# Loading K and V of a decode attention in rows of 32 KB instead of 16 KB per partition

## The chip, the cores and the metric

The kernel runs on one core of one Trainium2 chip. The metric is device time in microseconds (us) of one execution; the profile's span is about 2 us shorter than that time. Inputs and weights are bf16.

## The reference

Two decode attentions, A and B, each of one token, are computed and their outputs put side by side. A looks at the last 2048 positions of its cache, B at all 8192.

```python
B, Sq, D = 1, 1, 576
Hq, Hkv, Sk, Dh = 32, 16, 8192, 128          # two query heads share a K/V head
# x [1,1,576], k_cache and v_cache [1,16,8192,128], wq [576,4096], wo [4096,576], for A and for B
W = min(4096, max(256, Sk // 4))             # 2048, for A only
q = (x @ wq) in heads;  k, v = the caches (A: only the last W positions)
p = softmax(q k^T * Dh ** -0.5);  o = p v
out = o in one row @ wo                      # [1,1,576] for A, the same for B, concatenated
```

The work is moving bytes: 8 MB each of K and V for A, 32 MB each for B, and 18 MB of weights; in all 102.76 MB have to come out of HBM. (Sizes of arrays, slots and rows are in units of 1024: 98 such MB are 102.76 million bytes. The profile's totals and GB/s are in units of 1000.)

## The kernel before

SP (SyncE) issues all large loads, in order. K and V have four slots each; a slot holds 16 KB in each of 128 partitions (2 MB). A slot for B holds two heads, 64 rows of HBM each, a row being 64 positions of one head (16 KB in one piece); for A four heads and 32 rows each. Neighbouring partitions belong to different heads, so the load's source has the dimensions (row, head, bytes of a row): 64 x 2 for B, 32 x 4 for A.

```python
SLOT = 8192; NS = 4; TS = 64                 # elements of a slot in a partition; slots; positions of a row
G = [4, 2]                                   # heads of a slot: A, B

def load_kv(arrs, g, s, slots, name, after=()):
    ...
    ch = 128 // G[P] * TS
    def src():
        return arrs[P][0, i * G[P]:(i + 1) * G[P], r0:r0 + ch, :].rearrange("g (p t) d -> p g (t d)", t=TS)
    load(slots[:, s, :], src, [(name, s)], "%s%d" % (name, s), after)
```

PE (TensorE) transposes K in blocks of 128x128, ACT and DVE bring them to SBUF (`kt`), PE multiplies them with the queries. Columns of `kt` of different heads alternate, so the products read every second column:

```python
def k_scores(g, u, place):                   # one half slot, 1 MB of K
    for e in range(2):
        for j in range(4):
            rhs = kt[:, u % NKT, j * 1024:(j + 1) * 1024].rearrange("d (x g) -> d x g", g=2)[:, :, e]
            pe.matmul(sacc[32 * j:32 * j + 32, 512 * half:512 * half + 512], lhsT=qst[...], rhs=rhs, ...)
```

Then follow softmax of a chunk, its transposes, the products with V out of the V slots, and at the end the product with wo. A K slot is free for its next load when it is transposed; a V slot when its products are done, which needs the chunk's softmax. `x` arrives in two small loads issued by ACT.

## Time and profile before

| | before |
|---|---|
| time, median of 4 runs | 249.97 us |
| span of the profiled run | 247.7 us |
| bytes, rate over the span | 102.76 MB, 415 GB/s |
| busy: PE, ACT, DVE | 68%, 35%, 33% |

Five lines of the page of the kernel before. The first three divide the span into 40 slices: the granted clock of TensorE in tenths, the mean busy share of the 16 DMA engines in tenths (9 is 90% or more), and GB/s. Then all packets, and the queue that carries SP's loads with the share of 16 engines' span that its packets took.

```profile
PEclk9999959999799979998899955999858755557555
DMA  7999999999999999999999999999999999999993
GB/s 270 406 433 431 430 431 421 426 423 429 431 425 429 426 421 431 422 431 434 423 429 429 423 431 429 426 437 426 429 429 423 431 426 429 434 427 427 421 406 138
DMA packets 8235, 102.92 MB, mean 416 GB/s; under 512 B 1184, under 2 KB 1312, under 8 KB 2080
...
q1 hardware_dynamic: 7936, 102.77, 98.0%
```

All DMA engines are busy from the second slice to the last but one, at 421 to 437 GB/s in nearly every slice. That is the bound.

The costliest groups of PE in the kernel before, by form (count | busy us, mean ns of one | idle before and what ended it):

```profile
L466 PE MATMUL ktps<-ident,kslots 128*128 128x128 bf16 x1280 | 85.1, 230 | 12.4 <-PEq L214 12.4
L557 PE MATMUL opsum<-vslots,ptm 128*32 128x128 bf16 x1280 | 28.1, 262 | 28.0 <-PEq L214 23.7 <-issue 4.3
L486 PE MATMUL sacc<-kt,qst 128*32 128x512 bf16 x320 | 25.3, 392 | 1.8 <-PEq L214 1.8
```

The issues of the kernel before, from the DMA view (count, KB each, median us from issue to landing):

```profile
kslots<-in_B_k_cache_dram SPq DMA_DIRECT2D x16, 2048.0 KB, 19.6
vslots<-in_B_v_cache_dram SPq DMA_DIRECT2D x16, 2048.0 KB, 18.4
```

At the 428 GB/s of the stretch from 100 to 200 us, a 2 MB load (2.10 million bytes) moves in 4.9 us, so a load issued 19 us before it lands has three others ahead of it: the queue is never near empty.

The trace also holds a record of every DMA packet (start, duration, bytes, queue). Wherever this document gives packet times, they are summed up from these records. One row of a partition is one packet. Before, 5632 packets of 16384 bytes (5120 of K and V, 512 of wq) took 614 ns in the median, 616.9 on average, and the engines lacked data for only 0.4 us between the first and the last data packet.

### The profile page before, as it was taken

The numbers are of one execution on the slowest core, as the hardware profiler recorded it, in microseconds if no ns is written. First come the engines' busy times: TensorE is split into PE (matmuls) and PEld (weight loads), VectorE is DVE, ScalarE is ACT, GpSimd is POOL, SyncE is SP. The second block draws the span as 40 slices with busy tenths as digits, with TensorE's granted clock in tenths as the row PEclk, the third lists the DMA queues.
The fourth block names the chain that finished last, engine by engine and source line by source line (L and its number), as shares of the span: only waits on it lengthen the run. The fifth ranks groups of instructions, "written<-read, shape, count | busy, mean of one in ns | idle before, by whom it ended". The sixth has DMA issues, their size and how long they took to land. (4 is left out here: it accounts for less than half of the span.)

```text
span 247.7 us, 7505 instructions
## 1 busy us (share of the span) xinstructions
PE 169.6 (68%) x3406; PEld 132.3 (53%) x3406; DVE 81.0 (33%) x152; ACT 87.1 (35%) x92; POOL 12.9 (5%) x49
## 2 busy tenths in 40 slices
PE   0193589994999559995999638998345144685634
PEld 0031288763877458864878428785244142584522
DVE  0001225554555017564555122655004004204000
ACT  2000047767478009786578004775200000000000
POOL 7501000000000000000000000000000000000000
PEclk9999959999799979998899955999858755557555
DMA  7999999999999999999999999999999999999993
GB/s 270 406 433 431 430 431 421 426 423 429 431 425 429 426 421 431 422 431 434 423 429 429 423 431 429 426 437 426 429 429 423 431 426 429 434 427 427 421 406 138
DMA packets 8235, 102.92 MB, mean 416 GB/s; under 512 B 1184, under 2 KB 1312, under 8 KB 2080
## 3 DMA queue, kind: packets, MB, share of 16 engines
q1 hardware_dynamic: 7936, 102.77, 98.0%
q8 instruction: 8, 0.13, 0.2%
q10 hardware_dynamic: 288, 0.00, 0.1%
q14 instruction: 3, 0.02, 0.0%
HBM read 102.76 MB, written 0.00 MB: 415 GB/s over the span
## 5 line engine op out<-in xcount | busy, mean ns | idle before, releaser
L472 ACT ACTIVATE kt<-ktps 128x1024 bf16<-128x1024 bf16 x80 | 77.9, 1021 | 54.5 <-PE ktps L466 54.4
L466 PEld LDWEIGHTS ktps<-ident,kslots 128*128 128x128 bf16 x1280 | 78.9, 103 | 27.9 <-issue 27.9
L466 PE MATMUL ktps<-ident,kslots 128*128 128x128 bf16 x1280 | 85.1, 230 | 12.4 <-PEq L214 12.4
L475 DVE COPY kt<-ktps 128x1024 bf16<-128x1024 bf16 x80 | 55.2, 691 | 53.7 <-PE ktps L466 53.6
L557 PE MATMUL opsum<-vslots,ptm 128*32 128x128 bf16 x1280 | 28.1, 262 | 28.0 <-PEq L214 23.7
L557 PEld LDWEIGHTS opsum<-vslots,ptm 128*32 128x32 bf16 x1280 | 25.3, 119 | 31.6 <-issue 31.6
L486 PE MATMUL sacc<-kt,qst 128*32 128x512 bf16 x320 | 25.3, 392 | 1.8 <-PEq L214 1.8
L566 DVE TENSOR_TENSOR diag<-opsum,rows 128x512 f32<-128x512 f32 x5 | 3.5, 691 | 55.9 <-PE opsum L557 55.9
L425 PE MATMUL opsum<-vslots,xpad 128*32 128x512 bf16 x64 | 8.2, 489 | 14.8 <-DVE xpad L410 12.1
L599 ACT ACTIVATE stat<-stat 128x1 f32<-128x1 f32 (+1 forms) x2 | 0.6, 294 | 37.2 <-DVE stat L597 37.2
L425 PEld LDWEIGHTS opsum<-vslots,xpad 128*32 128x32 bf16 x64 | 2.3, 119 | 17.6 <-issue 13.1
L457 POOL COPY qst<-qtm 128x64 bf16<-128x64 bf16 x20 | 4.5, 236 | 123.2 <-PE sacc L486 113.5
L646 PE MATMUL ktps<-kslots,opj 128*32 128x144 bf16 x184 | 6.1, 326 | 5.8 <-DMA kslots<-in_B_wo_dram 3.9
L486 PEld LDWEIGHTS sacc<-kt,qst 128*32 128x32 bf16 x320 | 5.1, 94 | 8.2 <-issue 4.4
L431 ACT ACTIVATE qrow<-opsum 128x512 bf16<-128x512 f32 x2 | 1.2, 597 | 23.1 <-PE misc L425 23.1
L523 ACT ACTIVATE psb<-sacc,stat 128x2048 bf16<-128x2048 f32 x3 | 5.9, 1967 | 8.5 <-DVE stat L517 8.5
L646 PEld LDWEIGHTS ktps<-kslots,opj 128*32 128x32 bf16 x184 | 5.2, 145 | 6.4 <-DMA kslots<-in_B_wo_dram 4.2
L425 PE MATMUL misc<-vslots,xpad 128*32 128x512 bf16 x64 | 8.2, 487 | 0.0
L630 PE MATMUL misc<-acc,pick 128*128 128x32 f32 x16 | 3.8, 404 | 3.6 <-DVE acc L624 2.9
L433 DVE CAST qrow<-misc 128x512 bf16<-128x512 f32 x2 | 1.4, 692 | 14.6 <-PE misc L425 14.6
L652 DVE CAST outsb<-ktps 128x144 bf16<-128x144 f32 x2 | 0.6, 307 | 16.0 <-PE ktps L646 16.0
L630 PEld LDWEIGHTS misc<-acc,pick 128*128 128x128 f32 x16 | 3.6, 328 | 3.8 <-DVE acc L624 3.0
(66 smaller groups left out, 62.1 us busy)
## 6 DMA issues: line engine op xcount, KB each, us to landing
kslots<-in_B_k_cache_dram SPq DMA_DIRECT2D x16, 2048.0 KB, 19.6
vslots<-in_B_v_cache_dram SPq DMA_DIRECT2D x16, 2048.0 KB, 18.4
kslots<-in_A_k_cache_dram SPq DMA_DIRECT2D x4, 2048.0 KB, 29.8
vslots<-in_A_v_cache_dram SPq DMA_DIRECT2D x4, 2048.0 KB, 23.5
vslots<-in_A_wq_dram SPq DMA_DIRECT2D x2, 2048.0 KB, 9.9
vslots<-in_B_wq_dram SPq DMA_DIRECT2D x2, 2048.0 KB, 19.6
kslots<-in_A_wo_dram SPq DMA_DIRECT2D x2, 2016.0 KB, 23.8
kslots<-in_B_wo_dram SPq DMA_DIRECT2D x1, 2016.0 KB, 31.2
```

The source lines that it names most:

```text
L425: ins = pe.matmul(qps[c][32 * j:32 * j + 32, :], lhsT=xpad[:, P, x, :], rhs=src[:, o:o + 512], start=(u == 0), stop=(u == WQ_UNITS - 1))
L433: add("dve", lambda dve: dve.tensor_copy(qrow[:, 512:1024], misc[:, :]), reads=[B_M], writes=[("qrow", 1)])
L457: add("pool", lambda pool: pool.tensor_copy(qst[:, s * 64:(s + 1) * 64], qtm[:, o:o + 64]), reads=[("qtm", KIND[g])], writes=[("qst", s)], ...
L466: ins = pe.matmul(ktps_bf[q][:, t * 128:(t + 1) * 128], lhsT=kslots[:, s, o:o + 128], rhs=ident[:, :], start=True, stop=True, is_transpose ...
L472: add("act", lambda act, q=q, dst=dst: act.activation(dst, ktps_bf[q], ACT.Copy), reads=[("bank", q)], writes=[("kt", u % NKT, q)], tag="e ...
L475: add("dve", lambda dve, q=q, dst=dst: dve.tensor_copy(dst, ktps_bf[q]), reads=[("bank", q)], writes=[("kt", u % NKT, q)], tag="e%d%d" % ( ...
L486: ins = pe.matmul(sacc[32 * j:32 * j + 32, 512 * half:512 * half + 512], lhsT=qst[:, s * 64 + e * 32:s * 64 + e * 32 + 32], rhs=rhs, start ...
L523: return act.activation(psb[:, :].rearrange("p (x g) -> p x g", g=2), src, ACT.Exp, bias=st(P, C_NB + k), scale=SCALE, accum_out=st(P, C_L ...
L557: ins = pe.matmul(opsum[32 * j:32 * j + 32, s * DH:(s + 1) * DH], lhsT=ptm[:, o:o + 32], rhs=vslots[:, s, b * 128:(b + 1) * 128], start=(u ...
L566: return dve.tensor_tensor(diag[:, g % 2, :, :], opsum[:, :].rearrange("p (s d) -> p d s", s=NS), m, ALU.mult)
L630: ins = pe.matmul(misc[:, 0:32], lhsT=pick[:, r, :], rhs=acc[:, d, 32 * r:32 * r + 32], start=(r == 0), stop=(r == 3))
L646: ins = pe.matmul(ktps[P][32 * j:32 * j + 32, 0:OUTW], lhsT=opj[:, P, jj:jj + 32], rhs=view[:, o:o + OUTW], start=(jj == 0), stop=(jj == H ...
```

## The change

A packet costs a little more than its bytes (before, 178 ns for 4608 bytes and 614 ns for 16384, in the median), so longer rows should be cheaper. The change goes to 128 positions (32 KB) for each row and halves the number of packets. To keep the chunks small it takes eight heads into a slot, 16 rows of each; there are two slots for K and two for V, of 4 MB each. wq comes in rows of 36 KB, one load for A and one for B. The chunks of A and B have the same shape, which removes masks and zeroing. The eight heads of a slot are sorted out by extra products ("spread") that write P^T in the form the V products need.

The core of the diff (cut):

```diff
-SLOT = 8192
+SLOT = 16384
-NS = 4
+NS = 2
+NG = 8
-TS = 64
+TS = 128
+CH = 128 // NG * TS
 ...
-            return arrs[P][0, i * G[P]:(i + 1) * G[P], r0:r0 + ch, :].rearrange("g (p t) d -> p g (t d)", t=TS)
+            return arrs[P][0, s * NG:(s + 1) * NG, r0:r0 + CH, :].rearrange("g (p t) d -> p g (t d)", t=TS)
 ...
-            for e in range(2):
+            for g in range(NG):
                 for j in range(4):
-                    rhs = kt[:, u % NKT, j * 1024:(j + 1) * 1024].rearrange("d (x g) -> d x g", g=2)[:, :, e]
+                    o = k0 * UNIT + j * 2048
+                    rhs = kt[:, o:o + 2048].rearrange("d (x g) -> d x g", g=NG)[:, :, g]
 ...
+    def softmax_spread(i, loop):
+        pe.matmul(dst[:, :], lhsT=spread[:, i, :], rhs=pt0[:, :], ...)      # eight for each chunk
+        dve.tensor_tensor(<ptm>, <dst>, <hmask>, ALU.mult)
 ...
+    ORDER = [                                   # order of issue: K, V slots and wo
+        [("k", 0), ("k", 1), ("v", 0)],
+        [("k", 2), ("k", 3), ("v", 1)],
+        [("k", 4), ("v", 2), ("k", 5), ("v", 3)],
 ...
```

## The prediction

> **What bounds it now.** The DMA engines. The page's slices show them at 90% or more from the second slice on; the main queue's packets took 98.0% of 16 engines' span. In the trace's packet records the 16 engines have data in flight for 242.3 us of the 242.7 us between first and last data packet: no starvation. PE (68%), ACT (35%) and DVE (33%) matter only where they free a slot late. The chain of waits ends in B_wo's load.
>
> **What it can gain.** Only cost per packet. Median packet times: 4608 B 178 ns, 9216 B 352 ns, 16384 B 614 ns: a line of 7.4 ns + 0.0370 ns per byte. By it (estimates) 32768 B takes 1221 ns instead of 2 x 614, 36864 B takes 1373 ns. Over all K, V, wq and wo rows, with fewer completion packets, that is about 1.7 us less per engine (0.7%). [...]this trace already runs at 421 to 437 per slice, so over 2% is out of reach.
>
> **What it can lose: an empty queue.** Before, 2 MB loads are issued a median 18 to 20 us before they land. After, 4 MB loads (9.8 us each) go into four slots; slots come free later, and SP issues in order. Release against need:
>
> - x: its packets came one per 0.61 us data packet on each engine. Behind 36 KB packets both x need about 25-30 us (estimate; 14.1 before), so the B query ends at about 37 us. Slot k0 is ready at 35-36 us: costs PE 1-2 us, not the DMA.
> - K stage: a 1 MB transpose unit takes 1.96 us PE, 2 x 1.02 us ACT, 2 x 0.69 us DVE. The eight spread evictions (0.69 us each, like the 128x512 TENSOR_TENSOR) make two units DVE-bound, about 4.2 us each. A K stage is then 26-27 us, in 39 us of DMA.
> - Chunk 1's round: PE work is continuous there; V slot 0 is released about 28 us after the first K lands, and its refill is needed just then. No margin. A first-pass instruction fetch, like the 4.3 us "issue" wait in the middle of V before, falls here: 0-6 us idle, say 2.
> - Later chunks: 3-4 us of margin, none lost.
> - First wo load: reuses K slot 0, but is issued after K slot 1's last transposes (9.3 us after landing, 10-11 if PE is cold), while only one 9.8 us load is queued behind that K. Issue to first packet takes 1 us: 1-2.5 us idle. [...]64 transposes took 6.5 us at 31.9 us, 4.05 at 91.8.
>
> PE, ACT and DVE savings are off the critical path. The tail (3 us) stays.
>
> **Sum.** 249.9 - 1.7 + about 3 idle = 251.2 us; 80% range 248.2 to 255. Faster by over 2%: 1%; within 2%: 88%; slower by over 2%: 11%.
>
> **Right if** packets of 32768 B take about 1.22 us, busy engine time falls 1.5-2 us, and the DMA row dips near 95 us and near 205 us. **Wrong if** there is no dip (then about 248.2), if large packets are no cheaper per byte, if instruction fetches behind 32 KB packets take much longer, or if the late x starves the early K loads (then 255 or more).

Two clauses are cut from it, as they did not come from this case's runs. Neither held a term of the sum, which stays 249.9 - 1.7 + about 3 = 251.2 us; but "over 2% is out of reach" now rests on the estimated 0.7% alone. What some of its words stand for in the trace of the kernel before: "cold" is a granted clock of 0.54 over the 64 transposes that took 6.5 us, against 0.92 over those that took 4.05; the "completion packets" are taken to be the 888 packets of 4 bytes in the queue of SP's loads, 9 ns each (488 after); and the 1 us from issue to first packet is the first load, issued at 0.73 us, with its first data packet at 1.75.

## More of the kernel before

The score products (L486) keep PE busy for 25.3 us in all. They overlap one another (320 of 392 ns would make 125 us), so the mean of one says less than the busy time.

## The result, and the profile after

| | before | after |
|---|---|---|
| time, median of 4 runs | 249.97 us | 450.2 us (444.81 to 454.31) |
| ratio of the fast runs | | 1.794, 95% interval 1.777 to 1.810 |
| span of the profiled run | 247.7 us | 446.9 us |
| packets of K and V (before: with 512 of wq): count, mean | 16384 bytes: 5632, 0.617 us | 32768 bytes: 2560, 2.43 us |
| wq packets of 36864 bytes | none | 256, median 1.364 us |

The ratio is the mean time of the fast runs of one kernel over that of the other's of the same rounds, so not quite the ratio of the medians in the table. One run of the kernel after (454.31 us) is slow and left out of it.

The same lines of the page of the kernel after:

```profile
PEclk9978698795999659757975965797596579856566
DMA  9999999999999999999999999999999998899994
GB/s 360 432 241 218 205 224 199 224 201 223 221 220 214 226 220 209 229 226 214 217 224 211 214 232 202 223 217 214 223 214 217 226 214 268 204 209 214 204 389 170
DMA packets 4636, 102.94 MB, mean 230 GB/s; under 512 B 784, under 2 KB 912, under 8 KB 1296
...
q1 hardware_dynamic: 4336, 102.76, 97.8%
```

The engines are as busy as before, and move half as much: 430 GB/s while wq comes in (the second slice), about 215 GB/s as soon as K does, 389 again at the end when only wo is left. A busy DMA engine is an engine with a packet under way, not an engine at its rate: the DMA row alone would have called this kernel healthy, and the GB/s row beneath it shows the fault at a glance.

PE's costliest groups in the kernel after, by form:

```profile
L470 PE MATMUL ktps<-ident,kv 128*128 128x128 bf16 x1280 | 101.6, 248 | 128.2 <-PEq L215 121.3 <-issue 6.8
L495 PE MATMUL sacc<-kt,qst 128*32 128x256 bf16 x640 | 75.6, 632 | 0.0
L550 PE MATMUL opsum<-kv,ptm 128*32 128x128 bf16 x1280 | 24.6, 247 | 34.0 <-PEq L215 24.0 <-issue 9.9
```

A second surprise: the score products (L495) move as many columns as before (640 x 256 against 320 x 512) and take 75.6 us instead of 25.3.

The issues of the kernel after, from its page:

```profile
kv<-in_B_k_cache_dram SPq DMA_DIRECT2D x8, 4096.0 KB, 53.1
kv<-in_B_v_cache_dram SPq DMA_DIRECT2D x8, 4096.0 KB, 40.4
```

Where the 200 us went is a simple sum over the packet records. K and V now take 2560 packets of 2428 ns where twice 616.9 ns was the old price of the same bytes: 2560 x (2428 - 1234) ns / 16 engines = 191 us. Engines without a packet between first and last data grew from 0.4 to 5.3 us, 5 us more. wo rows that shared the queue with the last V loads are about 3 us slower for each engine (16128 bytes 707 ns on average against 606 before, 20736 bytes 959 where the line of the prediction gives 775). So the question is why a packet of 32768 bytes takes 2.43 us, when one of 36864 bytes, in the same run, takes 1.36.

### The profile page after: what moved, and what is told of

It reads as the page before. It is cut to its first block, busy times and chain, and to the rows that moved or that the text cites. A ratio compares the mean times of both kernels' runs of the same rounds, so it can differ in the third digit from the quotient of the medians.

```text
span 446.9 us, 8083 instructions
## 1 busy us (share of the span) xinstructions
PE 236.4 (53%) x3716; PEld 159.6 (36%) x3716; DVE 101.7 (23%) x197; ACT 86.8 (19%) x96; POOL 15.4 (3%) x41
## 5 line engine op out<-in xcount | busy, mean ns | idle before, releaser
L470 PE MATMUL ktps<-ident,kv 128*128 128x128 bf16 x1280 | 101.6, 248 | 128.2 <-PEq L215 121.3
L470 PEld LDWEIGHTS ktps<-ident,kv 128*128 128x128 bf16 x1280 | 95.4, 114 | 142.8 <-issue 139.2
L495 PE MATMUL sacc<-kt,qst 128*32 128x256 bf16 x640 | 75.6, 632 | 0.0
L550 PE MATMUL opsum<-kv,ptm 128*32 128x128 bf16 x1280 | 24.6, 247 | 34.0 <-PEq L215 24.0
L550 PEld LDWEIGHTS opsum<-kv,ptm 128*32 128x32 bf16 x1280 | 23.5, 112 | 37.0 <-issue 37.0
L495 PEld LDWEIGHTS sacc<-kt,qst 128*32 128x32 bf16 x640 | 20.4, 113 | 43.0 <-issue 42.0
L430 PE MATMUL opsum<-kv,xpad 128*32 128x512 bf16 x72 | 9.7, 514 | 24.2 <-DVE xpad L415 24.2
L540 DVE TENSOR_TENSOR ptm<-misc,hmask 128x512 bf16<-128x512 f32 x24 | 16.4, 682 | 3.5 <-PE misc L534 3.3
L540 DVE TENSOR_TENSOR ptm<-ptps,hmask 128x512 bf16<-128x512 f32 x24 | 16.3, 678 | 0.0
L534 PE MATMUL misc<-pt,spread 128*128 128x512 bf16 x24 | 9.6, 398 | 4.2 <-PEq L215 2.7
```

Source lines behind the costliest of these rows:

```text
L430: ins = pe.matmul(qps[c][32 * j:32 * j + 32, :], lhsT=xpad[:, P, x, :], rhs=src[:, o:o + 512], start=(u == 0), stop=(u == WQ_UNITS - 1))
L470: ins = pe.matmul(ktps_bf[q][:, t * 128:(t + 1) * 128], lhsT=kslots[s][:, o:o + 128], rhs=ident[:, :], start=True, stop=True, is_transpose ...
L495: ins = pe.matmul(sacc[32 * j:32 * j + 32, 256 * h:256 * h + 256], lhsT=qst[:, s * 256 + g * 32:s * 256 + g * 32 + 32], rhs=rhs, start=(a ...
L534: add("pe", lambda pe: pe.matmul(dst[:, :], lhsT=spread[:, i, :], rhs=pt0[:, :], start=True, stop=True), reads=["pt0", "spread"], writes=[ ...
L540: return dve.tensor_tensor(to, dst[:, :].rearrange("p (f n h) -> p f n h", f=4, n=4), m, ALU.mult)
L550: ins = pe.matmul(opsum[32 * j:32 * j + 32, s * DH:(s + 1) * DH], lhsT=ptm[:, o:o + 32], rhs=vslots[s][:, b * 128:(b + 1) * 128], start=(m ...
```

## The experiments

All are single looks (one timed run and a profile each, so their state is unknown), as nearly every question here is one of tens of per cent; the kernel before, run beside each of them, gave 249.63 to 250.04 us. Kernels "wrong on purpose" read other data than they should, for the sake of the timing. One more caution: the comparison with the reference cannot see every error in this problem. The kernel of `e5_flat_only` below pairs scores with the wrong keys and was still reported as correct. That fits scores so small that softmax is nearly flat, but no run here measured that. And the theories speak of which rows an engine moves and in what order; that is assumed throughout, as the packet records name no engine.

### 1. Address pattern, packet size, or number of heads

`m1_sweep` has no computation, only loads from one cache in 21 patterns:

```python
for dims, row, gap, off in TESTS:              # dims: the source's outer dimensions, outermost first
    for r in range(4):                         # four loads, then wait for all of them
        sp.dma_start(<buffer r, 128 partitions>, <source with dims, row>)
    sp.wait_ge(s_dma, n)
```

> No computation, wrong output on purpose: 21 address patterns, each four loads of about 4 MB, one pattern after the other, only the packet records count. Measured after the change: 32768-byte packets took 2.43 us on average instead of the 1.22 us predicted, and the 36864-byte packets of wq took 1.36 us, their predicted time. Theory A (address spacing): the 16 engines start their rows 32 KB apart in HBM and read 32 KB on[...]; then the pattern as after repeats about 2.5 us; a row spacing of 36 KB, and probably 33 or 34 KB, brings 1.22 us for the same packet size; and the same addresses read in 16 KB pieces stay slow (about 1.2 us a piece instead of 0.61). Theory B (packet size): a 32768-byte packet is itself slow; then every pattern with 32 KB packets takes about 2.5 us, whatever the spacing, and the 16 KB pieces of the same addresses take 0.61 us. Theory C (eight heads 2 MB apart, one after the other on an engine): then a head spacing of 2 MB + 4 KB or of 512 KB brings 1.22 us and 36 KB row spacing alone does not.

The kernel had a slip: its unit was half of what was meant, so all rows and row spacings were half as long as the text says (16 KB for "32 KB"); the head spacing of 2 MB was right. The comparison between patterns does not suffer. Some of the 21, with the real sizes:

| source: outer dimensions, row | spacing of rows; of heads | packet, median | rate |
|---|---|---|---|
| 16 x 8, 16 KB | 16 KB; 2 MB | 1276 ns | 212 GB/s |
| the same addresses, in pieces of 8 KB | 16 KB; 2 MB | 614 ns | 219 GB/s |
| 16 x 8, 8 KB | 16 KB; 2 MB | 612 ns | 223 GB/s |
| 16 x 8, 16 KB | 18 KB; 2 MB | 1265 ns | 212 GB/s |
| 16 x 8, 16 KB | 64 KB; 2 MB | 1255 ns | 212 GB/s |
| 16 x 8, 16 KB | 16 KB; 2 MB + 4 KB | 1274 ns | 211 GB/s |
| 16 x 8, 16 KB | 16 KB; 256 KB (all contiguous) | 1273 ns | 214 GB/s |
| 32 x 4, 16 KB | 16 KB; 2 MB | 611 ns | 412 GB/s |
| 64 x 2, 8 KB | 8 KB; 2 MB | 309 ns | 392 GB/s |
| 128, 16 KB | 16 KB | 611 ns | 402 GB/s |

All three theories fall. Neither the size of the packets, nor the spacing of rows, nor that of heads brought any of the slow patterns out of 210 to 226 GB/s. All 16 slow patterns have 16 as the source's outermost dimension; the five fast ones have 32, 64 or 128.

In `e1_half_rows` each slot is filled by two loads of 16 KB rows:

```diff
-        load(slots[s], src, [(name, s)], "%s%d" % (name, s), after)
+        def halves(sp):
+            a, d = src(), slots[s]
+            return [sp.dma_start(d[:, h * 8192:(h + 1) * 8192], a[:, :, h * 8192:(h + 1) * 8192]) for h in range(2)]
```

> The kernel after the change, with each K or V slot filled by two loads of 16 KB per partition (first halves of all rows, then second halves), correct result. Theory B (packet size) expects 16384-byte packets of 0.61 us and about 250 us in all. Theory A (spacing) leaves it open: rows still stand 32 KB apart but an engine reads only 16 KB before it changes the head, as the A loads of the kernel before did at full rate; if the overlap of 16 KB is still too regular it expects 1.2 us packets and about 450 us.

Correct, 425.0 us; packets of 16384 bytes took 1193 ns in the median, against 614 before. Packet size is not the cause. (The A loads of the kernel before, which the text names, ran at 421 to 431 GB/s between 25 and 65 us.)

`e2_pitch36` takes rows 36 KB apart:

```diff
-            return arrs[P][0, s * NG:(s + 1) * NG, r0:r0 + CH, :].rearrange("g (p t) d -> p g (t d)", t=TS)
+            return bass.AP(..., ap=[[18 * 512, 16], [SK * DH, NG], [1, TS * DH]])    # elements; wrong on purpose
```

> The kernel after the change with the 16 rows of a head taken 36 KB apart instead of 32 KB (wrong result on purpose: rows overlap other rows and some keys are left out), packets of 32768 bytes kept. Theory A (spacing): packets of about 1.22 us, and the time the prediction gave, 248 to 255 us. Theories B (packet size) and C (heads 2 MB apart): about 450 us still.

453.6 us and packets of 2500 ns: no help. Theory A was a supposition that no run had shown. Here rows 36 KB apart are as slow as rows 32 KB apart (2500 ns against 2495 in the kernel after, in the median), and in `m1_sweep` heads 2 MB + 4 KB apart as slow as heads 2 MB apart (1274 ns against 1276), so it is out.

### 2. Which partitions the load writes

Theory D is the next supposition: packets that are written to certain partitions at the same moment hold one another up, and an outermost dimension of 16 brings such partitions together. Which partitions these are, and which engine writes them, was assumed; no run here shows it. The main test needs no such assumption: if the place of writing counts, one and the same source must run at different rates to different partitions. By rival E, to which the outermost dimension of 16 is slow in itself, it must not.

`m2_ports`, in the right units, and `e3_rows32`, the kernel after with other rows:

```diff
-            return arrs[P][0, s * NG:(s + 1) * NG, r0:r0 + CH, :].rearrange("g (p t) d -> p g (t d)", t=TS)
+            r1 = min(r0, SK - 2 * CH)           # wrong on purpose: 32 rows of four heads
+            return arrs[P][0, s * NG:s * NG + 4, r1:r1 + 2 * CH, :].rearrange("g (p t) d -> p g (t d)", t=TS)
```

In `m2_ports`, s is the step from one written partition to the next, for 16 rows of one and the same source. In its last pattern two small loads, of 16 and 48 rows, go ahead of the 16 x 8 loads and are meant to put the engines out of step.

> No computation, wrong output on purpose; only the packet records count, with packets of 32768 bytes (16384 in one pattern). The first sweep dropped theories A, B and C: only patterns whose source has an outermost dimension of 16 were slow. Theory D[...]. It expects: loads of 16 x 8 rows 2.44 us a packet and about 215 GB/s at row spacings of 32 and 36 KB; 32 x 4, 64 x 2 and 128 rows 1.22 us and over 400 GB/s. [...] Last, [...]16 x 8 loads take 1.22 us a packet although nothing of their pattern differs from the first. Rival E (the outermost dimension of 16 slows the source side or the descriptor generation): the step of the destination makes no difference, s=1 to 8 are all alike, and being out of step does not help.

| load, packets of 32768 bytes | packet, median | rate |
|---|---|---|
| 16 x 8 rows, 32 KB apart | 2549 ns | 211 GB/s |
| 16 x 8 rows, 36 KB apart | 2542 ns | 209 GB/s |
| 32 x 4, 64 x 2, 128 rows | 1213 ns each | 423 to 424 GB/s |
| 16 rows to partitions 0, 1, 2, ... | 4816 ns | 112 GB/s |
| 16 rows to partitions 0, 2, 4, ... | 2554 ns | 207 GB/s |
| 16 rows to partitions 0, 4, 8, ... | 2564 ns | 201 GB/s |
| 16 rows to partitions 0, 8, 16, ... | 2560 ns | 205 GB/s |
| 16 rows to partitions 0, 7, 14, ... | 2474 ns | 215 GB/s |
| 16 rows to partitions 0, 3, 6, ... | 4260 ns | 126 GB/s |
| 16 x 8 rows, behind the two small loads | 2238 ns (from 1213) | 242 GB/s |

From one and the same source the destination alone moves the rate from 112 to about 207 GB/s, so here the place of writing sets it, and the rival is out. A step of 1 costs a factor of four over the 1213 ns of the fast loads (4816 ns), steps of 2, 4 and 8 a factor of two (2554 to 2564 ns). But three expectations were missed. For the steps of 7 and 3, by median and rate (2474 ns and 215 GB/s, 4260 ns and 126 GB/s), nearly all were slow. And the two small loads helped only in part: 79 of 576 packets took less than 1.3 us, 308 more than 2.2.

`m4_base` was made to settle this with nothing changed but where the same 64 partitions begin:

```python
for base in (0, 32, 64, 16, 28, 36, 0, 32):
    for r in range(5):                           # 16 rows of 32 KB of four heads
        load(r, base, [(1, 64)], <offset>, [(32 * KB, 16), (HEAD, 4)], 32 * KB)
    sp.wait_ge(s_dma, n[0])
```

> No computation, wrong output on purpose: one and the same load (16 rows of 32 KB of four heads, outermost dimension 16[...]), to 64 neighbouring partitions that begin at 0, 32, 64, 16, 28, 36, and again 0 and 32. Theory D[...]: from 0 and from 64 [...]packets of 2.44 us and about 210 GB/s; from 32 [...]packets of 1.22 us and over 400 GB/s, though the outermost dimension is still 16. Rival E (the outermost dimension of 16 by itself is slow): all bases alike at 2.4 us. [...]

That theory D had 0 and 64 slow and 32 fast came from the assumption; the times are measured.

| first partition | packet, median | time for 10 MB | rate |
|---|---|---|---|
| 0 (and again) | 2560 (2547) ns | 51.1 (50.8) us | 205 (207) GB/s |
| 64 | 2562 ns | 51.2 us | 205 GB/s |
| 16 | 2559 ns | 51.0 us | 206 GB/s |
| 28 | 1213 ns, slowest 2461 | 47.8 us | 219 GB/s |
| 36 | 1213 ns, slowest 2509 | 49.0 us | 214 GB/s |
| 32 (and again) | 1213 (1213) ns | 25.1 (25.1) us | 418 (417) GB/s |

This is the cleanest result. The source, the shape, the number of partitions and the outermost dimension of 16 are the same in all rows, and moving the destination by 32 partitions doubles the speed. From 28 and from 36 most packets keep their 1213 ns, and the load ends when a few slow ones do: at base 28, 38 of 320 packets took over 2 us, and in the last two slices of that load (9.25 us each) the page shows 25 and 28 GB/s with the DMA row at 1 tenth, about two packets of 2.46 us at a time (an estimate from these numbers). From 16 practically every packet is slow, as from 0: 320 packets of 2559 ns in 16 engines make 51.2 us, and the load took 51.0. So the place of writing is shown as the cause; which packets hold up which, and how, is not.

One step stays inferred. `m4_base` writes 64 partitions; the 16 x 8 loads go to all 128. That those are slow because packets meet at the same moment is theory D's reading of their being slow with 16 and fast with 32, 64 or 128 outermost (211 GB/s against 423 to 424, `m2_ports`). The one test that was meant to vary the moment alone, putting engines out of step, gained 15% (211 to 242 GB/s) where theory D expected about a doubling.

> The kernel after the change, each slot loaded with 32 rows of 32 KB of four heads instead of 16 rows of eight (wrong result on purpose, all else kept: bytes, packet size, issue order, waits, computation). Theory D[...]: packets of 1.22 us, and the time that the prediction gave for the whole change, 248 to 255 us, with the DMA gaps it named near 95 and 205 us. Rival E also expects this, as the outermost dimension is 32; a theory that puts the loss on anything else in the change (instruction fetch, buffers, x, PE) expects it to stay near 450 us.

The packets were right at once: 1213 ns in the median, 1235 on average. The time was not: 291.8 us, 41.8 us of it with engines idle. The lines of the page of `e3_rows32`:

```profile
DMA  8999999974999604999991899993999919799993
GB/s 321 412 422 437 432 434 434 432 301 165 434 431 430 280 2 147 435 434 434 434 434 54 380 434 434 434 434 145 360 434 434 434 77 366 289 430 431 401 408 141
```

At full rate (434 GB/s) the kernel has holes in its queue once in each chunk, up to a whole slice: slots come free too late. Something the slow packets had hidden now bounds the kernel.

And the converse. `e6_before_16x8` forces the old kernel into the new shape:

```diff
-            return arrs[P][0, i * G[P]:(i + 1) * G[P], r0:r0 + ch, :].rearrange("g (p t) d -> p g (t d)", t=TS)
+            h, r1 = i % 2 * 8, min(r0, SK - 16 * TS)     # wrong on purpose: 16 rows of eight heads
+            return arrs[P][0, h:h + 8, r1:r1 + 16 * TS, :].rearrange("g (p t) d -> p g (t d)", t=TS)
```

> The converse: the kernel before, each of its 2 MB loads taken as 16 rows of 16 KB of eight heads (wrong result on purpose), all else kept: packet size, four slots, order, computation. Theory D: packets of 16384 bytes take about 1.2 us instead of 0.61 and the time goes to 430 to 455 us. If the slowdown needs anything else of the change, it stays near 250 us.

423.6 us, a little under the expected range; packets of 16384 bytes took 1182 ns in the median. Its page:

```profile
DMA  8999999999999999999999999999999999999994
GB/s 319 427 296 216 211 219 222 224 216 225 228 244 230 244 224 231 233 227 224 225 224 222 224 224 232 235 230 242 232 238 239 233 247 228 246 244 228 323 415 171
```

The shape of the load alone, in a kernel that is otherwise the one before, produces the slowdown.

### 3. The second cause: products that read every eighth column

In `e3_rows32` PE's lines show what held the slots. Two lines of its timeline (start, us, what, count), in the first round of B:

```profile
91.29 3.79 PE L472 MATMUL ktps<-ident,kv 128*128 128x128 bf16 x64
95.02 3.83 PE L497 MATMUL sacc<-kt,qst 128*32 128x256 bf16 x32
```

The products of 2 MB of K take as long (3.8 us) as its transposes. Before, the same bytes took two groups of 0.63 us. `e4_rows32_flat` and `e5_flat_only` take the step away, with and without the fast loads:

```diff
-                    rhs = kt[:, o:o + 2048].rearrange("d (x g) -> d x g", g=NG)[:, :, g]
+                    rhs = kt[:, o + 256 * g:o + 256 * g + 256]       # wrong on purpose
```

> The 32-row loads of the run before (packets at full speed) and, in addition, the score products read 256 neighbouring columns of K transposed instead of every eighth (wrong result on purpose). In the run before, a group of 32 such products took 3.75 us, where the prediction had allowed about 1 us, and the DMA stood idle for 41.8 us. Theory F: these 2.7 us, four times in each of five chunks, are what held the slots back; then this run loses the DMA gaps and comes to what the prediction gave, 248 to 255 us, with DMA idle of a few us. Rival: the slots are late for another reason (coarse slots and order of issue alone); then it stays near 290 us.

256.5 us, 35 us less than `e3_rows32` and 1.5 us above the expected range. Engines idled for 8.2 us instead of 41.8. The remaining holes, in its page:

```profile
DMA  7999999999999968999999999999999949998992
GB/s 278 464 406 419 440 448 428 410 440 420 366 439 448 417 291 332 455 448 417 412 453 448 417 412 453 448 417 410 443 438 438 412 158 429 422 470 387 434 408 104
```

They lie near 95 us and near 205 us (slices of 6.36 us), where the prediction had put them. The timeline of `e4_rows32_flat` shows the first: V products stop in the middle, with nothing in the profile to wait for.

```profile
88.53 1.91 PE L553 MATMUL opsum<-kv,ptm 128*32 128x128 bf16 x123
94.68 4.01 PE L553 MATMUL opsum<-kv,ptm 128*32 128x128 bf16 x133 [4.24 <-issue]
```

The whole group lists 4.2 us of such waiting, so it happens in the first pass through this code alone. The packet records hold one packet of 16384 bytes of the kind `instruction` at 92.3 to 93.3 us, inside this wait, and one at 86.7 to 87.8 us inside the 4.3 us wait of the kernel before (84.9 to 89.2 us). So an instruction fetch is the likely cause; no run took it away.

> The kernel after the change, loads untouched, only the score products read neighbouring columns (wrong result on purpose). Theory D: [...]the packets still take about 2.4 us and the time stays at 435 to 452 us. A theory in which the slow products hold the loads back in the kernel as it is expects a gain of tens of us.

457.6 us (one run), 5.6 us above the range: no gain at all, although the products were three and a half times quicker:

```profile
L496 PE MATMUL sacc<-kt,qst 128*32 128x256 bf16 x640 | 21.1, 276 | 0.0
```

Packets still took 2499 ns in the median. So in the kernel as changed the products cost nothing, and the slow loads all. The four cases side by side:

| | every eighth column | neighbouring columns |
|---|---|---|
| loads 16 x 8 | 450.2 us (the change) | 457.6 us |
| loads 32 x 4 | 291.8 us | 256.5 us |

`m3_steps` measures the products alone:

```python
rhs = kt[:, o:o + 256 * step].rearrange("d (x g) -> d x g", g=step)[:, :, 0]     # step 1, 2, 4, 8, 16
pe.matmul(dst[32 * j:32 * j + 32, 0:256], lhsT=qst[:, 0:32], rhs=rhs, ...)        # j = 0 to 3 in turn, 32 times
```

> No loads and wrong output on purpose: score-like products alone (32 weight columns, 256 moving columns, four column groups in turn), 128 of each with moving elements 1, 2, 4, 8 and 16 apart (2 to 32 bytes). Theory F[...]: 1, 2 and 4 alike, about 0.03 us a product, 8 and 16 about 0.118 us, as in the kernel after the change. If the step is not the cause (weight loads of 32 columns, the accumulation, PSUM), all five are alike.

The groups of `m3_steps`, one for each step (stepa is 1, stepb 2, stepc 4, stepd 8, stepe 16):

```profile
L37 PE MATMUL stepe<-kt,qst 128*32 128x256 bf16 x128 | 15.0, 641 | 0.0
L37 PE MATMUL stepd<-kt,qst 128*32 128x256 bf16 x128 | 14.7, 631 | 0.0
...
L37 PE MATMUL stepc<-kt,qst 128*32 128x256 bf16 x128 | 7.5, 407 | 0.0
L37 PE MATMUL stepb<-kt,qst 128*32 128x256 bf16 x128 | 3.8, 275 | 0.0
L37 PE MATMUL stepa<-kt,qst 128*32 128x256 bf16 x128 | 3.7, 272 | 0.0
```

Busy time over 128 products gives 0.029 us a product at steps of 1 and 2, 0.059 at 4, 0.115 at 8 and 0.117 at 16. The expectation held at 8 and 16, and missed at 4: a step of 4 elements (8 bytes) already doubles the time (7.5 us against 3.7). That 1, 2 and 4 would be alike was not shown by any run before.

## Why the prediction was wrong

Predicted 251.2 us, 80% range 248.2 to 255; measured 450.2.

- **"What bounds it now. The DMA engines.": right**, and still so after the change.
- **The step that failed: "By it (estimates) 32768 B takes 1221 ns instead of 2 x 614".** This term, summed over all rows, was worth -1.7 us; for K and V alone it measured +191 us: 2428 ns on average. The line through the packet times was good, as packets of 32768 bytes take 1213 ns wherever the load ran at over 400 GB/s (`m2_ports`, `m4_base`) and the 36864-byte packets of wq took 1364 ns (1373 predicted). But the old packet times held for loads with 32, 64 or 128 as outermost dimension. The change made it 16, and packets took twice as long (2549 ns against 1213 in `m2_ports`); that this is because other partitions are then written at the same moment is theory D's supposition. The prediction treated the source's shape as mere layout.
- **"A K stage is then 26-27 us": wrong too, but without effect in the kernel as changed.** In the trace of the kernel after it took 38 us (106.0 to 143.7 us), 2.2 us of it a wait that ended after the stage's second slot had landed. With loads at full rate it took 34.6 us (`e3_rows32`, 75.2 to 109.7 us), and 22.7 us with neighbouring columns (`e4_rows32_flat`, 65.8 to 88.5 us). The term at fault is the score products, which the prediction did not price anew; at a step of eight columns a group of 32 takes 3.75 us, not about 1. With the loads at full rate this alone brought 291.8 us, still far outside the range.
- **Holes in the queue: right in place, somewhat small in size,** once both errors are taken out. `e4_rows32_flat` shows 2.8 us near 95 us (2 predicted) and 3.4 us near 205 us (1 to 2.5 predicted). Its engines are busy for 241.3 us with data instead of 242.3: 1.0 us gained, against 1.7 predicted. It ends at 256.5 us, 5 us above the prediction. In the kernel as changed these holes do not show.
- **x behind the large packets: right, or nearly.** The second x landed at 30.8 us (25-30 predicted, 14.1 before); its packets started 16 in each 0.61 us before, 16 in each 1.36 us after, behind the wq packets of 1364 ns.
- **The warning "large packets are no cheaper per byte" was the right one to give**, but the prediction weighed it as a matter of per cents and had no case for a factor of two.

Three things stay open. Which engine writes which partitions was not seen, as the packet records name no engine. Why 64 partitions from 0, 16 or 64 on are slow as a whole, from 28 on in 38 of 320 packets and from 32 on not at all (`m4_base`), and why steps of 7 and 3 slow nearly all packets (`m2_ports`), was not found. And no correct kernel that beats the old one came out: by the packets of `m2_ports`, 32 KB rows are worth 1213 ns instead of 2 x 611 for the same bytes, 0.7% of the K and V time, and `e4_rows32_flat`, with both faults out and a wrong result, is still slower than before, as its queue runs dry twice.

## What to carry to other kernels

Before changing a load's access pattern, time the load alone with its new shape and its destination, not only with the new length of a row: an outermost dimension of exactly 16 over 128 partitions halved the rate here (211 GB/s), 32, 64 and 128 did not (423 to 424), and one and the same load ran at 205 GB/s to the partitions from 0 on and at 418 from 32 on. Read GB/s next to DMA busy; a full DMA row says nothing about the rate. And when heads or groups are interleaved more finely, price the step at which later products read the result: here 2 elements were free (3.8 us against 3.7), 4 cost twice (7.5), 8 four times as much (14.7).
